# Gated complex linear attention and a relu-squared MLP: the first 32 keys of a chunk are multiplied together with the state, and the order of steps is a written table

## The chip, the cores and the metric

The kernel runs on one core of one Trainium2 chip. The metric is the device time of one execution in microseconds (us); lower is better. A core has four compute engines that run side by side, each in its own order: TensorE (PE, matrix products into PSUM; its weight loads appear as PEld), VectorE (DVE), ScalarE (ACT) and GpSimd (POOL). SyncE (SP) only issues transfers; ACT and POOL issue some as well. Within one engine instructions run strictly in order, so one that waits holds up all behind it.

## What is computed

For 4 batches and 8 heads, over 768 steps, a complex state of 48x48 decays by a complex gate, takes in k v^T and is read by q. The result, as 3072 tokens of 384 values, goes through a two-layer MLP. All of it is fp32.

```python
scale = np.minimum(mag, 0.999) / (mag + 1e-06)      # mag = |a|
a_re_n, a_im_n = (a_re * scale, a_im * scale)
for t in range(S):
    new_re = ar * S_re - ai * S_im
    new_im = ar * S_im + ai * S_re
    kv = np.einsum('bhd,bhe->bhde', k[:, :, t], v[:, :, t])
    S_re, S_im = (new_re + kv, new_im)
    y[:, :, t] = np.einsum('bhd,bhde->bhe', q[:, :, t], S_re)
...
h = x @ w_in                  # 3072x384 by 384x2048
r = np.maximum(h, 0.0)
return (r * r) @ w_out        # 2048x384
```

## The kernel before

The work is cut into six units n of 512 tokens, each a stretch of one batch for all 8 heads; a unit has four chunks j of 128 steps, and its heads go in four pairs i. A batch has 768 steps, so units 0 and 3 begin one (they have no state at their first chunk; the code calls them fresh), units 1 and 4 contain a beginning (no state at chunk 2; cross), and units 2 and 5 have a state at all four chunks.

For each unit DVE and ACT normalise the gates, run a scan over them and scale q and k (the chain: lines 1070 to 1509), with transfers L1546 that gather K into the tiles KC. Then, for every pair:

- turn or turn_pe: Q and K are transposed into the tile QT, whose 96 rows are 48 real and 48 imaginary parts. The first pairs use PE for that (L1624, with ACT copies L1628), the others DVE transposes (L1598) and transfers.
- score: PE multiplies K by Q for each chunk (L1645), and DVE multiplies the scores by a causal mask, from PSUM into a tile A (also called xn and e), in one instruction for each head (L1648, 512 elements a partition).
- keep: PE forms each chunk's sum of k v^T (L1676); DVE adds it to the state before (L1690), or ACT copies it where there is none (L1686). States within a unit lie in St, those between units in S, both 96 rows high.
- mix: the output of a chunk is masked scores times v, plus Q times the state. PE runs the two heads of a pair side by side in two column groups (L1707, L1711), and ACT copies the result to yt (L1720); transfers on SP put it into xT (L1733), where it is the input of the MLP.

The MLP of a unit is dense: products with w_in (L1758), relu and square on ACT (L1791, L1792), products with w_out (L1806 in unit 0). From unit 1 on the second product works on half-sized matrices (L1869) that DVE prepares and adds up (L1885, L1894), and the results leave from POOL's queue (L1824), the last ones from SP's and ACT's. In the last unit a part of the first product is in L2014. The weights arrive early as integers of their own bit pattern and are taken apart and converted in pieces on ACT (L947, L952) and DVE (L954, L958, L961). Products named fill (L1564) have no use for the result.

The order on each engine is decided before the kernel is built, by the class Plan. Every piece above is a step, registered by step(engine, duration, reads, writes, function, rank). Plan.order plays the steps through with the registered durations and takes, for each engine, the ready step with the lowest rank. A table SHIFTS changes the ranks of some steps, and constants make PE's steps wait a margin and group the narrow products. The part of mix that matters here:

```python
for j in js:
    for h in range(2):
        pe.matmul(ps[64 * h:64 * h + D, j - js[0]], lhsT=v5[:, j, 2 * i + h],
                  rhs=aa[h][:, j], start=True, stop=at[j] is None)
    for h in range(2):
        if at[j] is not None:
            pe.matmul(ps[64 * h:64 * h + D, j - js[0]], lhsT=at[j][:, h],
                      rhs=T[:, j, 0, h], start=False, stop=True)
```

A second, general path stands behind a flag; it doesn't run for this input.

Of the kernel before, what the change touches and what calls it, by code (L numbers as in the profile page):

```python
# [481 lines left out]
class Plan:  # L482
# [3 lines left out]
    MARGIN = 0.3  # L486
    SLACK = 1.7
# [9 lines left out]
    SHIFTS = {  # L497
        -1193.0: (320,),
        -802.0: (1256,),
        -595.0: (2284,),  # L500
        -594.0: (2285,),
        -500.0: (2041,),
        -301.0: (2694,),
        -210.0: (2688,),
        -108.0: (2690,),
        -100.0: (range(14, 17), 25, 37, 107, range(109, 111), 113, 166, 321, 344, 346, 356, 396,
            range(575, 577), 579, 625, range(1086, 1088), range(1245, 1247), 1271, 1304, 1306,
            1588, 1824, 1826, 2117, 2691, 2697, 2708, 2716,),
        100.0: (9, 11, range(20, 22), 24, 41, 104, 210, 234, 272, 279, 284, 304, 306, 314, 327,
            329, 331, 352, 354, 373, 375, 377, 379, 406, 408, range(410, 412), 417, 422, 424,  # L510
            range(431, 433), 440, range(443, 445), 448, range(452, 454), 466, 482, 496, 507, 564,
            range(681, 683), range(684, 686), 781, 783, 788, 800, 809, range(811, 814), 865, 869,
            885, 942, 1057, range(1116, 1118), 1123, 1129, 1132, 1146, 1164, range(1175, 1177),
            1188, range(1259, 1261), 1320, 1323, 1328, 1331, 1338, 1340, 1348, 1355, 1377, 1381,
            1384, 1389, 1392, 1406, 1478, 1480, 1729, 1737, 1740, 1748, 1763, 1781, 1792, 1794,
            range(1797, 1799), 1813, 1847, 1856, 1998, range(2043, 2045), 2071, 2073, 2135, 2147,
            2155, range(2163, 2165), 2180, range(2192, 2194), 2242, 2371, 2433,
            range(2445, 2447), range(2450, 2452), range(2456, 2458), 2459, 2472, 2474, 2545,
            2578, 2581, 2592, 2633,),
        189.0: (1283,),  # L520
        197.0: (2079,),
        200.0: (871,),
        292.0: (2097,),
        293.0: (2094,),
        302.0: (2233,),
        389.0: (2557,),
        503.0: (1815,),
        504.0: (1416,),
        588.0: (1405,),
        597.0: (1827,),  # L530
        602.0: (range(1665, 1668),),
        703.0: (1821,),
        793.0: (1345,),
        802.0: (2552,),
        805.0: (2616,),
        898.0: (779,),
        903.0: (378,),
        911.0: (441,),
        996.0: (2546,),
        1009.0: (1852,),  # L540
        1016.0: (831,),
        1209.0: (403, 425,),
        1516.0: (458,),
        1717.0: (484,),
        3014.0: (1380,),
        3126.0: (879,),
        3128.0: (419,),
        3315.0: (1166,),
        3422.0: (893,),
        3520.0: (1190,),  # L550
        4109.0: (27,),
        7784.0: (407,),
        9674.0: (414,),
        11185.0: (31,),
        11579.0: (35,),
        12886.0: (402,),
        12982.0: (39,),
# [29 lines left out]

    def order(self):
        steps = self.steps
        rank = [100.0 * s[4][0] + s[4][1] for s in steps]  # L590
        for shift, which in self.SHIFTS.items():
            for ns in which:
                for n in [ns] if isinstance(ns, int) else ns:
                    rank[n] += shift
# [1582 lines left out]
```

## Time and profile before

| | |
|---|---|
| time, median of 3 runs | 655.2 us (654.69 to 655.5) |
| profiled execution | 652.32 us, span of its records 650.4 us |
| PE busy | 607.8 us (93%) |
| DVE busy | 585.2 us (90%) |
| ACT busy | 347.0 us (53%) |
| POOL busy | 122.0 us (19%) |
| mean granted PE clock | 0.991 |

The span is the time from the first record to the last. "Busy" counts compute instructions. A timeline row gives start, duration, engine, source line (L and a number), the operation with output<-inputs, and the number of records that it puts together, in brackets the idle time before it and what ended that; a group row gives total busy time and the mean of one in ns; the chain of waits gives, backwards from the end, which piece released which. A matrix product of fp32 shows as two records.

### The profile page before, as it was taken

What the parts mean: (1) busy time and instruction counts of PE and PEld (TensorE: products, weight loads), DVE (VectorE), ACT (ScalarE), POOL (GpSimd) and SP (SyncE); (2) the same over time, 40 slices, a digit from 0 to 9 for tenths busy, and PEclk for the clock granted to TensorE, in tenths of its full rate; (3) what the DMA queues carried; (4) which work ended last, traced back from release to release, by engine and by line L of the source; (5) the groups of instructions that cost most, each with busy time, mean ns of one, the idle gap of its engine ahead of it and who ended that gap; (6) DMA issues with size and microseconds to landing.
All of it is one profiled execution on the core that took longest, in us unless ns stands there. A gap on an engine that the chain in (4) does not pass through costs nothing.

```text
span 650.4 us, 12670 instructions
## 1 busy us (share of the span) xinstructions
PE 607.8 (93%) x4714; PEld 540.4 (83%) x4714; DVE 585.2 (90%) x1192; ACT 347.0 (53%) x635; POOL 122.0 (19%) x214
## 2 busy tenths in 40 slices
PE   0467999999999999999999999999999999999996
PEld 0356887688678988999989999989989989998996
DVE  7989999999998999998988999988998998459981
ACT  7479889888547244538353449354447442125500
POOL 7501140221100032040032030021040130051200
PEclk9979999999999999999999999999999999999999
DMA  6972787125620056452057580056370153377631
GB/s 210 298 268 50 162 220 202 42 50 147 174 53 1 1 126 163 127 156 41 7 144 176 128 182 2 13 138 177 101 183 0 26 132 92 82 240 270 213 116 30
DMA packets 55270, 80.39 MB, mean 124 GB/s; under 512 B 11392, under 2 KB 37920, under 8 KB 55200
## 3 DMA queue, kind: packets, MB, share of 16 engines
q0 software_dynamic: 15424, 42.12, 22.7%
q1 hardware_dynamic: 35168, 31.93, 19.3%
q10 hardware_dynamic: 4608, 5.44, 3.3%
q8 instruction: 39, 0.64, 0.4%
q14 instruction: 31, 0.25, 0.1%
HBM read 48.76 MB, written 4.72 MB: 82 GB/s over the span
## 4 chain that ended last, share of the span: by engine, by line
PE 72%; DVE 17%; DMA 5%; issue 2%; ACT 2%; POOL 0%; ACTq 0%; DVEq 0%; SPq 0%
PE d L1758 24%; PE d L1869 22%; PE d L1806 5%; PE sc L1645 4%; DVE f L1444 3%; PE yp L1707 3%; PE tr L1676 3%; PE yp L1711 2%; PE d L2014 2%; DMA w<-in_moe_w_in_dram 2%; PE tr L2014 2%; DVE g L1885 2%; DVE f L1509 2%; PE sc L2014 1%; DVE aq L1461 1%
## 5 line engine op out<-in xcount | busy, mean ns | idle before, releaser
L1758 PE MATMUL d<-xT,w 128*128 128x256 f32 x888 | 198.6, 380 | 1.5 <-DMA xT<-yt 1.2
L1758 PEld LDWEIGHTS d<-xT,w 128*128 128x128 f32 x888 | 167.3, 190 | 26.2 <-DMA xT<-yt 1.5
L1869 PE MATMUL d<-T,g 128*128 128x192 f32 x576 | 100.3, 329 | 0.3 <-DVE ot L1894 0.3
L1869 PEld LDWEIGHTS d<-T,g 128*128 128x128 f32 x576 | 93.6, 190 | 2.7 <-issue 1.1
L1791 ACT ACTIVATE g<-d 128x512 f32<-128x512 f32 x74 | 43.9, 593 | 69.9 <-PE d L1758 60.6
L1869 PE MATMUL d<-w,g 128*128 128x192 f32 x432 | 75.8, 328 | 0.0
L1869 PEld LDWEIGHTS d<-w,g 128*128 128x128 f32 x432 | 71.0, 190 | 1.2 <-ACT g L1791 0.2
L1824 POOL DMA_DIRECT2D out_dram<-ot x40 | 25.3, 638 | 218.4 <-DVE ot L1894 182.7
L1546 POOL DMA_DIRECT2D KC<-f x60 | 35.5, 600 | 112.2 <-DVE f L1509 82.6
L1885 DVE TENSOR_TENSOR g<-g 128x512 f32<-128x512 f32 x72 | 48.5, 684 | 7.6 <-ACT g L1792 4.4
L1792 ACT ACTIVATE g<-g 128x512 f32<-128x512 f32 x80 | 50.5, 631 | 2.5
L1444 DVE TENSOR_TENSOR f<-aq,xn 128x384 f32<-128x384 f32 (+1 forms) x72 | 46.8, 685 | 0.0
L1806 PE MATMUL d<-w,g 128*128 128x384 f32 x128 | 43.5, 489 | 0.2 <-DVE w L961 0.2
L1598 DVE STREAM_TRANSPOSE aq<-f 128x384 f32<-128x384 f32 (+1 forms) x51 | 42.2, 902 | 0.3
L1114 DVE TENSOR_TENSOR f<-aq 128x384 f32<-128x384 f32 x72 | 37.1, 552 | 0.5
L1645 PE MATMUL sc<-QT 96*64 96x64 f32 (+1 forms) x736 | 36.8, 249 | 0.5 <-ACT QT L1628 0.5
L1645 PEld LDWEIGHTS sc<-QT 96*64 96x64 f32 x736 | 34.2, 137 | 3.0 <-ACT QT L1628 1.2
L1806 PEld LDWEIGHTS d<-w,g 128*128 128x128 f32 x128 | 23.6, 190 | 15.4 <-DVE w L961 0.9
L1894 DVE TENSOR_TENSOR ot<-ot,d 128x192 f32<-128x192 f32 x70 | 23.3, 349 | 11.5 <-PE d L1869 11.2
L1475 ACT ACTIVATE f<-aq 128x768 f32<-128x768 f32 (+1 forms) x16 | 17.2, 1083 | 28.8 <-DVE aq L1461 28.7
L1037 POOL DMA_DIRECT2D v<-in_v_dram x30 | 23.2, 791 | 24.9 <-ACT f L1067 24.5
L1711 PE MATMUL yp<-QT,St 96*48 96x128 f32 x240 | 24.5, 272 | 0.0
(313 smaller groups left out, 1114.8 us busy)
## 6 DMA issues: line engine op xcount, KB each, us to landing
QT<-aq SPq DMA_DIRECT2D x136, 64.0 KB, 2.0
f<-in_moe_w_in_dram POOLq DMA_DIRECT2D x8, 768.0 KB, 8.1
f<-in_moe_w_out_dram POOLq DMA_DIRECT2D x8, 768.0 KB, 5.4
QT<-aq ACTq DMA_DIRECT2D x68, 64.0 KB, 2.3
KC<-f POOLq DMA_DIRECT2D x40, 96.0 KB, 3.4
out_dram<-ot POOLq DMA_DIRECT2D x40, 96.0 KB, 3.7
xT<-yt SPq DMA_DIRECT2D x34, 96.0 KB, 2.5
T<-in_moe_w_out_dram POOLq DMA_DIRECT2D x4, 768.0 KB, 11.0
```

The lines of the kernel that those rows point to most:

```text
L1114: lambda c=c, j=j: dve.tensor_tensor(out=f[:, j], in0=a[:, :, :, c - 1], in1=a[:, j, :, c].unsqueeze(1).to_broadcast([C, 2, HH, D]), op=AL ...
L1444: lambda j=j, r=r: dve.tensor_tensor(out=f4[:, j, r], in0=a[:, r], in1=over(j), op=ALU.mult), rk)
L1546: lambda i=i, p0=p0, m=m, src=src, queue=queue: queue.dma_start(out=kc[p0:p0 + m, i], in_=src),
L1598: lambda src=src, dst=dst: dve.transpose(out=dst, in_=src), rank)
L1645: pe.matmul(sa[p0:p0 + CH, j, t0:], lhsT=T[:, j, 1, h, t0:t0 + CH], rhs=T[:, j, 0, h, t0:], start=True, stop=True)
L1711: pe.matmul(ps[64 * h:64 * h + D, j - js[0]], lhsT=at[j][:, h], rhs=T[:, j, 0, h], start=False, stop=True)
L1758: pe.matmul(ps, lhsT=w1[:, f // FP, m, ts(f % FP, C)], rhs=xT[:, n % 2, m, ts(grp, G)], start=(m == 0), stop=(m == NM - 1))
L1791: act.activation(out=o, in_=ps, func=AF.Relu)
L1792: act.activation(out=o, in_=o, func=AF.Square)
L1806: pe.matmul(ps, lhsT=gt[:, f % 2, ts(i, C)], rhs=w2[:, f], start=(f == 0), stop=(f == NF - 1))
L1869: pe.matmul(bank[b][:, 0:DH], lhsT=gsets[x][h][:, j - HW * h, r], rhs=w(j), start=first and j == 0, stop=last and j == NT - 1)
L1885: lambda: dve.tensor_tensor(out=g[:, :, o], in0=g[:, :, x0], in1=g[:, :, x1], op=op),
```

## The change

**Near and far keys.** In a chunk of 128 steps the first 32 (QC) are taken apart. Their masked scores, 32 rows for each head and chunk, no longer go to A: DVE writes them into rows 96 to 127 of QT, right under Q. ACT copies v's rows of these 32 steps into rows 96 to 127 of St, under the state (two copies a pair), and of S (one a unit). One product over 128 rows then gives Q times state plus near scores times v. Where a chunk has no state, POOL sets those 96 rows to zero, so this product runs for every chunk (192 in place of 160 products). The product of the other scores with v is 96 columns wide in place of 128, since the keys after the first 32 reach only queries after the first 32. The mask multiply of a head is one of 384 elements a partition and two of 64 on 32 partitions.

For this the steps are laid out in 4 groups of 32 in place of 2 of 64 within a chunk, QT's order of columns changes, and each row block leaves by four transfers of 32 rows (in place of two of 64) on POOL's queue. POOL also clears QT's new rows.

**The order.** SHIFTS and the ranks' rules are gone; a table ORDER lists every engine's steps in order. Counts of steps: ACT 527 to 581, DVE 1172 to 1268, POOL 179 to 234, PE 575 and SP 286 as before.

```diff
-    MARGIN = 0.3
-    SLACK = 1.7
-    SETTLED, GROUP = 90.0, 8
-    HOLD, URGENT, FILL = {"DVE": 0.15, "ACT": 0.8}, (2, 0.2), (2, 0.2)
-    SHIFTS = {
-        -1193.0: (320,),
...
+    ORDER = {
+        "SP": """
+            220-222 2-3 1 0 5 7 223 4 225 6 224 226 14 13 15 9 18 20 19 17 229 228 227 8 16 12 11
...
+            heads = [(ready(e), line[e][head[e]], e) for e in line if head[e] < len(line[e])]
+            t, n, e = min(h for h in heads if h[0] is not None)
+            head[e] += 1
...
+    QC = C // 4
...
     def score(i, h):
-            step("DVE", tt(L), [(b,)], AK[a], lambda: dve.tensor_tensor(
-                out=As[a].rearrange("p (j o t) -> p j o t", o=2, t=C),
-                in0=bank[b].rearrange("p (j o t) -> p j o t", o=2, t=C), in1=mask4,
-                op=ALU.mult), rank)
+            step("DVE", tt(W * (C - QC)), [(b,)], AK[a], lambda: dve.tensor_tensor(
+                out=As[a][:, 0:W * (C - QC)].rearrange("p (j o t) -> p j o t", j=W // 2, o=2),
+                in0=sb4[:, :, :, QC:C], in1=far_mask, op=ALU.mult), rank)
+            for o in range(2):
+                step("DVE", tt(W * QC // 2), [(b,)], [("q0", s, h, o)],
+                     lambda o=o: dve.tensor_tensor(
+                         out=near[C - QC:C, :, o, h, 0, 0:QC], in0=sb4[CH * o:CH * o + QC, :, o, 0:QC],
+                         in1=mask2[CH * o:CH * o + QC, o, 0:QC].unsqueeze(1).to_broadcast(
+                             [QC, W // 2, QC]), op=ALU.mult), rank)
     def keep(i):
+            for o in range(2):
+                step("ACT", ac((1 + o) * 2 * D), [("v", vs(n))], [("sv", s, o)],
+                     lambda o=o, js_=js_, jv=jv: act.copy(
+                         out=sf[C - QC:C, js_], in_=v5[CH * o:CH * o + QC, jv, 2 * i:2 * i + 2]),
+                     rank)
+            if cross:
+                step("POOL", 0.2, [], [("st", s, 2)], lambda: pool.memset(st[:, 1], 0.0), rank)
     def mix(i):
                     for j in js:
                         for h in range(2):
-                            pe.matmul(ps[64 * h:64 * h + D, j - js[0]], lhsT=v5[:, j, 2 * i + h],
-                                      rhs=aa[h][:, j], start=True, stop=at[j] is None)
+                            pe.matmul(ps[64 * h:64 * h + D, j - js[0]], lhsT=at[j][:, h],
+                                      rhs=T[:, j, 0, h], start=True, stop=False)
                         for h in range(2):
-                            if at[j] is not None:
-                                pe.matmul(ps[64 * h:64 * h + D, j - js[0]], lhsT=at[j][:, h],
-                                          rhs=T[:, j, 0, h], start=False, stop=True)
+                            pe.matmul(ps[64 * h:64 * h + D, j - js[0], QC:C],
+                                      lhsT=v5[:, j, 2 * i + h], rhs=aa[h][:, j],
+                                      start=False, stop=True)
+                     + [("q0", got["T", i], h, o) for h in range(2) for o in range(2)]
+                     + [("sv", s, 0), ("sv", s, 1), ("Sv", n % 2)]
+        if which[0] == 0:
+            Sn = Sb[n % 2]
+            if fresh:
+                step("POOL", 0.4, [], [("S", n % 2, i) for i in range(NP)],
+                     lambda: pool.memset(Sn[0:R], 0.0), (CHAIN, 0.3) if n == 0 else rank)
+            step("ACT", ac(DM), [("v", vs(n))], [("Sv", n % 2)], lambda: act.copy(
+                out=Sn[C - QC:C].rearrange("p (h d) -> p h d", h=H), in_=v5[0:QC, 0]), rank)
     def rows(n, grp, i, o):
-        for p0 in (0, CH):
+        for p0 in range(0, C, QC):
```

**What the order is now.** Four places show it; in a row the source line comes first (numbers of the kernel that it belongs to), then the operation and output<-inputs. First DVE in unit 0, at the masks of pair 0. Before, L1648 is the mask, L1690 the state's addition, L1509, L1492 and L1500 the scaling of q and k of the next heads:

```order
L1509 TENSOR_TENSOR f_70<-f_70,yp 128x2x4x48
L1648 TENSOR_TENSOR A_90<-sc_115,mask 128x512
L1648 TENSOR_TENSOR A_91<-sc_116,mask 128x512
L1509 TENSOR_TENSOR f_70<-f_70,tr_118 128x2x4x48
L1509 TENSOR_TENSOR f_70<-aq_68,yp 128x2x4x48
L1690 TENSOR_TENSOR St_92<-tr_117,St_92 96x96
L1509 TENSOR_TENSOR f_70<-aq_68,tr_118 128x2x4x48
L1690 TENSOR_TENSOR St_92<-tr_117,St_92 96x96
L1492 SCALAR_TENSOR_TENSOR f_71<-f_71,lv 128x384
L1461 TENSOR_TENSOR aq_69<-f_71 128x384
L1500 SCALAR_TENSOR_TENSOR f_71<-f_71 128x384
L1509 TENSOR_TENSOR f_71<-f_71,aq_69 128x2x4x48 x2
```

After, on the same engine at the same masks (L1689 the far multiply, L1694 a near one, L1746 the state's addition, L995 and L988 conversions of w_in, L1548, L1535, L1531, L1539 and L1521 the scaling):

```order
L1548 TENSOR_TENSOR f_70<-aq_68,tr_118 128x2x4x48
L1521 TENSOR_TENSOR f_71<-f_71 128x384
L1689 TENSOR_TENSOR A_91<-sc_116,mask 128x384
L1548 TENSOR_TENSOR f_71<-f_71,aq_69 128x2x4x48
L1746 TENSOR_TENSOR St_92<-tr_117,St_92 96x96
L1548 TENSOR_TENSOR f_71<-f_71,aq_69 128x2x4x48
L1746 TENSOR_TENSOR St_92<-tr_117,St_92 96x96
L1694 TENSOR_TENSOR QT_74<-sc_116,mask 32x2x32
L1694 TENSOR_TENSOR QT_74<-sc_115,mask 32x2x32
L1689 TENSOR_TENSOR A_90<-sc_115,mask 128x384
L995 ISA w_66<-KC_77,w_66 128x1536
L1694 TENSOR_TENSOR QT_74<-sc_116,mask 32x2x32
```

The two masks of a pair, two neighbours before, are six multiplies with other work in between, and a conversion stands among them.

Second, ACT during unit 0's scan: L947 and L952 are conversions of w_in, L1222 copies of the scan that DVE waits for, L1416 and L1413 checks of the input. Before:

```order
L947 ACTIVATE w_67<-w_67 128x768 x2
L952 ACTIVATE w_67<-w_67 128x768
L1222 COPY yt_94<-e 128x4x24
L952 ACTIVATE w_67<-w_67 128x768
L1222 COPY yt_94<-yt_94 128x6
L1416 ACTIVATE junk,sums<-v_78 128x768
L1222 COPY A_90<-yt_94 128x6x4
L1413 ACTIVATE junk,sums<-aq_69 128x768
L1222 COPY yt_95<-A_90 128x2x24
```

After (L981 a conversion, L1261 the scan's copies, L1204, L1452, L1709 others; L1709 is a copy of v's rows under the state):

```order
L981 ACTIVATE w_67<-w_67 128x768
L1261 COPY yt_94<-e 128x4x24
L1261 COPY yt_94<-yt_94 128x6
L1204 COPY A_90<-tr_118 128x3
L1452 ACTIVATE junk,sums<-aq_68 128x768
L1261 COPY A_90<-yt_94 128x6x4
L1204 COPY A_90<-tr_117 128x3
L1261 COPY yt_95<-A_90 128x2x24
L1709 COPY St_92<-v_78 32x96
L1709 COPY St_93<-v_78 32x96
```

The two long conversions L952 no longer stand between the scan's copies.

Third, PE around the first dense product (L1758, d<-xT,w), which is followed by the last pair's mix. Before:

```order
L1676 MATMUL tr_117<-v_78,KC_77 33x48
L1676 MATMUL tr_117<-v_78,KC_77 64x48
L1676 MATMUL tr_117<-v_78,KC_77 33x48
L1758 MATMUL d_113<-xT,w_66 128x256
L1707 MATMUL tr_118<-A_90,v_78 48x128
L1707 MATMUL tr_118<-A_91,v_78 48x128
L1711 MATMUL tr_118<-QT_75,St_93 48x128 x2
L1707 MATMUL tr_118<-A_90,v_78 48x128
L1707 MATMUL tr_118<-A_91,v_78 48x128
L1711 MATMUL tr_118<-QT_75,St_93 48x128 x2
L1707 MATMUL yp<-A_90,v_78 48x128
L1707 MATMUL yp<-A_91,v_78 48x128
```

After (L1825 is the dense product, L1732 keep, L1764 and L1767 mix's two products):

```order
L1732 MATMUL tr_117<-v_78,KC_77 64x48
L1732 MATMUL tr_117<-v_78,KC_77 33x48
L1825 MATMUL d_113<-xT,w_66 128x256
L1825 MATMUL d_114<-xT,w_66 128x256
L1732 MATMUL tr_117<-v_78,KC_77 64x48
L1732 MATMUL tr_117<-v_78,KC_77 33x48
L1732 MATMUL tr_117<-v_78,KC_77 64x48
L1732 MATMUL tr_117<-v_78,KC_77 33x48
L1764 MATMUL yp<-QT_75,S_88 48x128 x2
L1767 MATMUL yp<-A_90,v_78 48x96
L1767 MATMUL yp<-A_91,v_78 48x96
L1764 MATMUL yp<-QT_75,St_93 48x128 x2
```

Two dense products stand ahead of the last pair's mix, where there was one; behind that mix PE went on with d_113 and the second part of xT, and now it goes on with one more product of the first part.

Fourth, PE in the last unit, at the narrow products of pair 2. Before, from the end of score (L1645) by a dense step (L1869) to mix:

```order
L1645 MATMUL sc_116<-QT_74 64x128 x2
L1645 MATMUL sc_116<-QT_74 64x64 x2
L1869 MATMUL d_112<-w_67,g 128x192 x8
L1707 MATMUL yp<-xn,v_78 48x128
L1707 MATMUL yp<-e,v_78 48x128
L1711 MATMUL yp<-QT_74,S_89 48x128 x2
L1707 MATMUL yp<-xn,v_78 48x128
L1707 MATMUL yp<-e,v_78 48x128
```

After (L1684 score, L1764 and L1767 mix), from the end of the next pair's score on:

```order
L1684 MATMUL sc_116<-QT_75 64x128 x2
L1684 MATMUL sc_116<-QT_75 64x64 x2
L1764 MATMUL yp<-QT_74,S_89 48x128 x2
L1767 MATMUL yp<-xn,v_78 48x96
L1767 MATMUL yp<-e,v_78 48x96
L1764 MATMUL yp<-QT_74,St_92 48x128 x2
L1767 MATMUL yp<-xn,v_78 48x96
L1767 MATMUL yp<-e,v_78 48x96
```

The dense step between score and mix is gone here, so two changes between wide and narrow products go. Over the whole program the changes from narrow to wide or back are 76 before and 66 after; after the first dense product, 62 and 52.

More of the change, by code (lines that the diff above doesn't have):

```diff
@@ L589, in order @@
         steps = self.steps
[L590 to L594, printed above, removed]
-        users = [[] for _ in steps]
-        left = []
-        for n, s in enumerate(steps):
-            left.append(len(s[2]))
-            for d in s[2]:
-                users[d].append(n)
-        engines = ("SP", "POOL", "PE", "DVE", "ACT")
@@ L602, in order @@
-        free = {e: 0.0 for e in engines}
-        wait = {e: [] for e in engines}
-        done, start, at = {}, {}, {}
+        line = {}
+        for e, text in self.ORDER.items():
+            own = sorted((n for n, s in enumerate(steps) if s[0] == e),
+                         key=lambda n: (steps[n][4], n))
+            line[e] = []
+            for part in text.split():
+                a, _, b = part.partition("-")
+                line[e] += own[int(a):int(b or a) + 1]
+            assert sorted(line[e]) == sorted(own)
@@ L605, in order, with ready @@
+        free = {e: 0.0 for e in line}
+        head = {e: 0 for e in line}
+        done, start = {}, {}
         bus = warm = 0.0
         tiled = False
+        flown = [], []
         def small(n):
             return any(x in steps[n][3].__qualname__ for x in self.SMALL)
-        def ready(n):
-            e = steps[n][0]
-            t = 0.0
+        def ready(e):
+            n, t = line[e][head[e]], free[e]
             for d in steps[n][2]:
-                same = steps[d][0] == e and steps[d][5] is None
+                if d not in done:
+                    return None
@@ L674, in order @@
                 done[n] = max(bus, t + dur) + lat
[L675 to L679 removed]
+                flown[e == "POOL"].append(done[n])
         self.start, self.done = start, done
@@ L804, in fast_path @@
     ypair = bank["yp"]
+    pool.memset(sums, 0.0)
     make_identity(nc, ident)
@@ L1315, in times @@
                 for r, op in ((0, ALU.subtract), (1, ALU.add)):
-                    step("DVE", 0.09, [(own, 0), (own, 1)], writes,
+                    step("DVE", 0.09, [(own, 0), (own, 1)] + I * (own == "H"), writes,
                          lambda r=r, op=op: dve.tensor_tensor(
@@ L2085, in fast_path @@
         if n == 0:
+            for s in range(2):
+                clear(s, (CHAIN, 0.3))
+        if n == 0:
             for i in range(NPIECE):
```

299 lines of the change are left out of this document (172 added, 127 removed).

## The prediction

> **What bounds the kernel.** I read the engines' busy shares and the chain first, then windows of 10 us, the long window of the middle, PE's waits, and then single instructions where the change works.
>
> ```profile
> PE 607.8 (93%) x4714; PEld 540.4 (83%) x4714; DVE 585.2 (90%) x1192; ACT 347.0 (53%) x635; POOL 122.0 (19%) x214
> PE 72%; DVE 17%; DMA 5%; issue 2%; ACT 2%; POOL 0%; ACTq 0%; DVEq 0%; SPq 0%
> 30.00:40.00 10.00, 3.45 (x16) 3.48 (x17) 8.21 (x34) 7.29 (x13) 1.58 (x3) 0.56 1.02 342
> 40.00:50.00 10.00, 8.11 (x34) 5.38 (x33) 9.91 (x25) 6.44 (x16) 0.00 (x0) 0.93 0.40 151
> 50.00:60.00 10.00, 7.70 (x93) 6.28 (x91) 9.97 (x21) 9.18 (x18) 1.12 (x2) 1.00 0.19 40
> 60.00:70.00 10.00, 8.63 (x134) 7.39 (x136) 9.86 (x25) 8.99 (x17) 2.15 (x4) 1.00 0.62 147
> 80.00:90.00 10.00, 8.75 (x77) 7.50 (x72) 9.93 (x15) 8.14 (x13) 4.10 (x7) 1.00 0.77 177
> 90.00:560.00 470.00, 469.06 (x3624) 415.30 (x3623) 439.26 (x893) 253.79 (x469) 77.11 (x124) 1.00 0.41 103
> 84.38 1.53 PE L1758 MATMUL d<-xT,w 128*128 128x256 f32 x6 [1.25 <-DMA xT<-yt]
> ```
>
> A window's columns are its length, then PE, weight loads, DVE, ACT and POOL busy, the granted clock and the DMA share. There are two regimes. From 90 to 560 us PE is busy 469.06 of 470 us: only a change in PE's own work counts there, and DVE has 30.7 us to spare, some 6 a unit. Before 90 us DVE is full (9.9 of 10) and PE stands idle, ending in the 1.25 us wait at the first dense products: there DVE's work counts. The profiled run took 652.32 us, 2.9 less than the median 655.2; I work out a difference on the profiled run and add it to the median.
>
> **PE's arithmetic in mix.** Twenty-four pairs have four chunks each: 96 chunk-pairs, 80 of them with a state (four of six units have one chunk without).
>
> ```profile
> 281.08 0.39 PE L1711 MATMUL yp<-QT,S 96*48 96x128 f32 x4
> 281.30 0.39 PE L1707 MATMUL yp<-A,v 128*48 128x128 f32 x4
> 281.52 0.39 PE L1711 MATMUL yp<-QT,St 96*48 96x128 f32 x4
> 282.40 0.39 PE L1711 MATMUL yp<-QT,St 96*48 96x128 f32 x4
> 282.72 0.59 PE L1869 MATMUL d<-T,g 128*128 128x192 f32 x2
> 57.41 1.56 PE L1645 MATMUL sc<-QT 96*64 96x128 f32 x32 [0.23 <-ACT QT L1628]
> 58.80 1.04 PE L1676 MATMUL tr<-v,KC 128*64 128x48 f32 x24
> L1707 PEld LDWEIGHTS yp<-A,v 128*48 128x48 f32 x184 | 10.8, 122 | 2.0 <-issue 1.7 <-ACT aq L1125 0.2
> ```
>
> One product of both heads follows the last by 0.22 us (281.08, 281.30, 281.52). Before: 96 x 0.22 + 80 x 0.22 = 38.7 us. After there are 96 state products, near scores included, still over 128 columns, and 96 far products over 96 columns. By columns a far one is 0.22 x 96/128 = 0.165. The score rows give a slower line: 32 records in 1.39 us, half at 128 columns (16 x 0.055 = 0.88), so one at 64 columns takes 0.032 against 0.055, four of them 0.128, and midway to 0.22 lies 0.174. I take 0.17: 96 x 0.39 = 37.4, **-1.3 us**. The ends: 0.128 as at 64 columns gives 33.4 (-5.3); no saving, since each product loads 48 weight columns in 122 ns whatever its width, gives 42.2 (+3.5). The score rows are nearer in kind and show width saved.
>
> **PE's order.** Wide products and these narrow ones alternate less often: counting after the first dense product, 62 changes of kind become 52. At 282.40 + 0.22 the next wide one could start at 282.62; it started at 282.72, so a change costs about 0.1 us: **-0.9 us** at 0.09 each (zero to -1.0). [...]
>
> **DVE.** Each of 48 scores has one multiply of 512 elements a partition; now one of 384 and two of 64.
>
> ```profile
> L1648 DVE TENSOR_TENSOR A<-sc,mask 128x512 f32<-128x512 f32 x28 | 18.3, 681 | 1.9 <-PE sc L1645 1.9
> L1509 DVE TENSOR_TENSOR f<-aq 128x384 f32<-128x384 f32 x20 | 10.5, 554 | 0.3
> L1690 DVE TENSOR_TENSOR St<-tr,St 96x96 f32<-96x96 f32 x32 | 7.7, 248 | 0.9 <-PE yp L1711 0.4
> 59.02 1.20 DVE A L1648 x2
> 61.44 0.46 DVE f L1509
> 61.27 0.17 DVE St L1690
> ```
>
> By durations: 554 + 2 x 0.9 of 248 (64 columns instead of 96, my estimate 220) - 681 = +0.31 us a score. But DVE overlaps neighbours: two full masks advance the chain by 1.20, a 384-wide one by 0.46, a 96x96 by 0.17, so +0.46 + 2 x 0.145 - 0.60 = +0.15. The chain is what counts: 48 x 0.15 = +7.2 us on DVE, against at worst 48 x 0.31 = 15. In the middle that lies under the 30.7 us of slack (1.2 to 2.5 a unit against 6), at nothing to the end; if the slack stands elsewhere than the masks, it becomes the slower rival. [...]
>
> **The lead.**
>
> ```profile
> 34.11 0.43 DVE L1197 TENSOR_TENSOR KC<-yt 128x96 f32<-128x96 f32 x2 [0.83 <-ACT yt L1222]
> 35.89 0.30 DVE L1197 TENSOR_TENSOR KC<-yt 128x36 f32<-128x36 f32 x2 [0.34 <-ACT yt L1222]
> 32.10 1.89 ACT L952 ACTIVATE w<-w 128x768 f16<-128x768 int16 x1
> L954 DVE TENSOR_SCALAR w<-w 128x768 uint32<-128x768 uint32 x5 | 2.8, 555 | 0.0
> L961 DVE CUSTOM_DVE_ANT_0 w<-w,w 128x1536 uint16<-128x1536 uint16 x3 | 2.9, 951 | 0.0
> L958 DVE SCALAR_TENSOR_TENSOR w<-w,w 128x768 uint32<-128x768 uint32 x1 | 1.0, 955 | 0.0
> L1070 DVE TENSOR_TENSOR f<-f 128x768 f32<-128x768 f32 x11 | 10.4, 948 | 2.2 <-ACT f L1067 2.2
> 65.83 0.29 SPq L1546
> 66.17 4.79 DMA KC<-f
> 79.78 4.35 DMA xT<-yt
> ```
>
> DVE's order up to the masks of pair 2 gains a conversion step L954 (0.47 of its 555), two L958 (+1.9, the row's 955 each), one L1070 (0.87), and 0.15 for each of six masks (+0.9); it loses two L961 (-1.74) and one L1690 (-0.17). That is +2.2. Against it, ACT's two conversions L952 no longer stand between the scan's side copies, for which DVE waits 0.83 and 0.34: -1.2. Three fewer instructions stand directly behind the one they depend on and so lose the overlap that the rows above show between a mean and its advance (681 and 600, 554 and 460, 248 and 170 ns, some 0.09 each): -0.3. DVE so hands over about 0.7 us later, and the delay goes on by the gather at 66.17, the state products and mix to the xT transfer that PE waits for. PE in turn does two more of the dense products ahead of that wait, 0.22 each (by the row at 84.38, 1.53 for six with the drain of the last in it): -0.4. Net **+0.3 us**. Bounds: +2.2 if neither gap nor spacing gives (a late weight transfer can hold ACT as before), -2.0 if the gaps go and the moved conversions fall into DVE's own waits.
>
> **Work at no cost to the end.**
>
> ```profile
> L1386 ACT COPY car<-ce 32x24 f32<-32x24 f32 x12 | 2.5, 208 | 0.2
> L1824 POOL DMA_DIRECT2D out_dram<-ot x40 | 25.3, 638 | 218.4 <-DVE ot L1894 182.7
> PE d L1806 <- DVE w L961: 0.2, 1, 0.2
> ```
>
> ACT gets 48 copies of 32 rows and six longer ones, at 208 ns for the nearest row some 10 to 12 us, about 2 a unit, under an engine idle for 47% (253.79 of 470 busy in the middle); uncovered, 0.2 a pair. They need v alone, which is there a unit early. POOL gets 40 more output issues of 0.64 us (+25 us) and about 13 small memsets, 0.1 each by its other memsets; POOL is busy 77.11 of 470 us, and its results go to memory, but an issue ahead of a gather on the same queue delays that by 0.64. The end of the kernel writes out on SP's and ACT's queues and is not touched. The mask and layout on POOL and in the transposes keep sizes. PE's stalls in the middle were 0.94 us; the largest, at the second product's weights, is 0.2 to 0.36, and conversions of those come earlier by DVE's order; but mix now also waits for three multiplies where it waited for one, with the dense products of the order queued behind it on PE, and ACT's relu behind those. I take these as even.
>
> **Sum.** -1.3 - 0.9 + 0.3 = -1.9 us: 650.4 for the profiled run, **653.3 us** beside the median 655.2.
>
> **Rivals.** *Slower: PE stands at mix for the small multiplies.* In the middle DVE is full in places.
>
> ```profile
> 181.00:234.00 53.00, 53.00 (x290) 46.88 (x287) 50.81 (x124) 23.32 (x50) 7.02 (x14) 1.00 0.10 23
> 407.00:421.00 14.00, 14.00 (x85) 13.69 (x84) 13.97 (x21) 4.28 (x6) 1.26 (x2) 1.00 0.04 10
> ```
>
> There DVE has 2.2 of 53 and 0.03 of 14 us free, and a written order lets nothing else go ahead of a waiting mix. If 0.31 a score, eight a unit, 2.5 us, reached PE in two or three units, +5 to +7.5 on -1.9 makes 658 to 661. It decides from 3.2 us of new waits on. Against it: PE waited 0.94 us in all that time, and mix needed its masks there as well. *The narrower product saves nothing*: +3.5 - 0.9 + 0.3 = +2.9, 658.1. *The clock stays low in the lead.*
>
> ```profile
> 36.97 4.60 PE L1564 MATMUL d<-ident 128*128 128x128 f32 x20
> 45.30 0.91 PE L1451 MATMUL sc<-f,A 128*128 128x384 f32 x2 [1.25 <-DVE f L1444]
> ```
>
> PE's clock averaged 0.56 from 30 to 40 and 0.93 from 40 to 50, so it rose to full at about 41.4, behind 4.6 us of filler products at 36.97; the new order leaves four of eleven there. If ten PE steps of 0.65 us, which run from 45.30 to 52.5, had to raise the clock themselves, 4.6 us of them at half rate would end them 2.3 later, where DVE takes their results from 53.98 on: +1.0 to +2.3 with that slack or without, so 654.3 to 655.6. [...]
>
> *The order gives more*: PE's idle time in the four windows from 40 us on that stand above was 6.8 us; half of it gone as well makes 649.9.
>
> **Chances.** Forecast 0.45 (its own range 651.7 to 654.6, four fifths of it below 653.9), more from the order 0.15, low clock 0.15 (within the bound), no saving by width 0.08, waits at mix 0.17. A measurement here tells 0.2%, 1.3 us. Faster: 0.36 + 0.15 + 0.02 = 0.53; slower: 0.08 + 0.15 = 0.23; same: the rest, 0.24. The range leaves out the ends of both far cases: 649.0 to 658.0.
>
> **What would show it.** Far products 0.17 apart in a mix of four chunks (1.56 us where it was 1.76); PE busy about 467 in a stretch that took 469; near multiplies at 0.2 us in DVE's rows; the scan's two gaps gone; first dense product within 0.5 us of 84.4. Wrong it is if PE shows waits on the near multiplies beyond 1 us in all, if far products keep 0.22, or if the lead's idle time moves by over 2 us.

## The result and the profile after

The changed kernel takes 659.32 us (658.62 to 659.59), beside 654.95 for the kernel before: 1.0065 times, 95% interval 1.0048 to 1.0083. It is slower, and my 653.3 was wrong by 6 us; the range to 658.0 did not hold it either. The profiled execution of after took 659.59 us (span 657.9), close to its median, while that of before was a short one (652.32), so a difference between the two traces overstates the loss by some 3 us. PE's stalls are better to compare: intervals from one product to the next that exceed the product's own pace by more than 0.15 us, after 88 us, sum to 2.0 us before and 8.6 us after.

The page's busy times and the chain, of after, answer the first two lines of the prediction:

```profile
PE 609.2 (93%) x4778; PEld 540.9 (82%) x4778; DVE 601.2 (91%) x1288; ACT 364.3 (55%) x689; POOL 153.0 (23%) x269
PE 46%; DVE 14%; DMA 2%; issue 2%; POOL 0%; ACT 0%; SPq 0%; DVEq 0%; ACTq 0%; POOLq 0%
```

The chain of after can be followed back only to 237 us from the start, so its shares sum to 64% and can't be set beside before's 72% and 17% as they stand; of what is listed, PE has 72% and DVE 22%. DVE is busy for 16 us more (601.2 against 585.2) with 96 more instructions. The long window of the middle, in the same columns as in the prediction:

```profile
90.00:560.00 470.00, 464.97 (x3634) 411.27 (x3634) 448.86 (x952) 273.26 (x518) 106.59 (x178) 1.00 0.42 104
```

PE lost 4.1 us of work there (464.97 against 469.06), in the stretch in which I let DVE's added time cost nothing. What PE waits for (total, times, longest), chosen lines of the view of waits:

```profile
PE yp L1764 <- DVE QT L1694: 1.9, 4, 0.9
PE tr L1732 <- DMA KC<-f: 1.3, 1, 1.3
PE d L1936 <- DVE g L1952: 1.1, 2, 0.7
PE d L1825 <- DVE ot L1961: 0.9, 2, 0.5
PE tr L1663 <- DVE St L1746: 0.8, 1, 0.8
PE sc L1684 <- DMA QT<-aq: 0.7, 1, 0.7
PE sc L1684 <- DVE T L1694: 0.5, 1, 0.5
```

Only 2.4 us (first and last line) are waits for the near multiplies themselves. The rest of DVE's lines are for g, ot and St, steps that the change did not touch: DVE as a whole is late.

DVE's rows show why. They are start, duration, line and shape, 176 to 181 us of after:

```profile
176.08 1.02 DVE L1153 TENSOR_TENSOR f<-aq 128x384 f32<-128x384 f32 x2
177.13 0.22 DVE L1694 TENSOR_TENSOR QT<-sc,mask 32x64 f32<-32x64 f32 x1
177.37 0.56 DVE L1689 TENSOR_TENSOR xn<-sc,mask 128x384 f32<-128x384 f32 x1
177.84 0.95 DVE L1109 TENSOR_TENSOR f<-f 128x768 f32<-128x768 f32 x1
178.82 0.22 DVE L1694 TENSOR_TENSOR QT<-sc,mask 32x64 f32<-32x64 f32 x1
179.05 0.36 DVE L1161 TENSOR_TENSOR aq<-f 128x192 f32<-128x192 f32 x1
179.43 0.45 DVE L1694 TENSOR_TENSOR QT<-sc,mask 32x64 f32<-32x64 f32 x2
179.91 0.25 DVE L1746 TENSOR_TENSOR St<-tr,S 96x96 f32<-96x96 f32 x1
180.09 0.34 DVE L1161 TENSOR_TENSOR aq<-f 128x192 f32<-128x192 f32 x1
```

Look at starts, not durations. The far multiply at 177.37 lasts 0.56 and its successor starts 0.47 later: overlapped. The 96x96 add at 179.91 lasts 0.25, its successor starts 0.18 later: overlapped. The near multiply at 177.13 lasts 0.22 and its successor starts 0.24 later: not overlapped. And what stands ahead of a near multiply loses its own overlap: L1109 at 177.84 lasts 0.95, and the near one starts 0.98 later. Over all 96, the median from a near multiply's start to the next start is 0.238 us, and the instruction ahead takes 0.11 longer to its successor than it otherwise does. So a near multiply among other instructions costs about 0.35 us of DVE's chain, where the prediction took 0.145; 22 of the 96 have another near one directly behind them, which saves them one 0.11.

### The profile page after: what moved, and what is told of

The parts are those of the page before. It is cut to its first block, busy times and chain, and to the rows that moved or that the text cites. A ratio compares the mean times of both kernels' runs of the same rounds, so it can differ in the third digit from the quotient of the medians.

```text
span 657.9 us, 13007 instructions
## 1 busy us (share of the span) xinstructions
PE 609.2 (93%) x4778; PEld 540.9 (82%) x4778; DVE 601.2 (91%) x1288; ACT 364.3 (55%) x689; POOL 153.0 (23%) x269
## 4 chain that ended last, share of the span: by engine, by line
PE 46%; DVE 14%; DMA 2%; issue 2%; POOL 0%; ACT 0%; SPq 0%; DVEq 0%; ACTq 0%; POOLq 0%
PE d L1825 19%; PE d L1936 18%; PE sc L1684 2%; DVE aq L1637 2%; PE d L2081 1%; DVE f L1153 1%; PE tr L2081 1%; PE yp L1764 1%; PE tr L1732 1%; DVE ot L1961 1%; DVE f L1548 1%; DVE aq L1133 1%; PE sc L2081 1%; DVE QT L1694 1%; DVE g L1952 1%
## 5 line engine op out<-in xcount | busy, mean ns | idle before, releaser
L1825 PE MATMUL d<-xT,w 128*128 128x256 f32 x888 | 197.7, 380 | 0.9 <-DVE ot L1961 0.9
L1825 PEld LDWEIGHTS d<-xT,w 128*128 128x128 f32 x888 | 167.6, 190 | 25.3 <-DVE ot L1961 1.7
L1891 POOL DMA_DIRECT2D out_dram<-ot x80 | 49.7, 624 | 132.5 <-DVE ot L1961 77.9
L1684 PE MATMUL sc<-QT 96*64 96x64 f32 (+1 forms) x736 | 39.0, 250 | 1.2 <-DMA QT<-aq 0.7
L1684 PEld LDWEIGHTS sc<-QT 96*64 96x64 f32 x736 | 35.3, 137 | 2.9 <-issue 1.0
L1764 PE MATMUL yp<-QT,St 128*48 128x128 f32 x268 | 28.1, 279 | 0.0
```

Of the source, the lines that this page charges most:

```text
L1684: pe.matmul(sa[p0:p0 + CH, j, t0:], lhsT=T[:, j, 1, h, t0:t0 + CH], rhs=T[:, j, 0, h, t0:], start=True, stop=True)
L1825: pe.matmul(ps, lhsT=w1[:, f // FP, m, ts(f % FP, C)], rhs=xT[:, n % 2, m, ts(grp, G)], start=(m == 0), stop=(m == NM - 1))
L1891: dma(pool, [("ot", o, 0), ("ot", o, 1)], [], lambda p0=p0: pool.dma_start(out=out[r + p0:r + p0 + QC, :].rearrange("(t c) e -> c t e", c= ...
```

## The experiments

All times are medians of five rounds beside the kernel before on the same chip (654.4 to 655.2 us in these rounds); the ratio to it and its 95% interval stand in brackets. Three kinds of questions: the lead, the order against the arithmetic, and then the near multiply itself.

**The lead.** In after, the state products ahead of the last mix of the lead waited for a gather which stood on SP's queue behind three loads and a transfer, though its input had long been there (its f at about 66.8 us; in sp_gather below it leaves at 67.78). SP's rows, start and duration:

```profile
74.80 1.70 SPq L1060 DMA_DIRECT2D aq<-in_a_re_dram  x2
76.55 0.60 SPq L1792 DMA_DIRECT2D xT<-yt  x1
77.20 0.59 SPq L1585 DMA_DIRECT2D KC<-f  x1
```

PE's rows behind it:

```profile
80.88 0.40 PE L1732 MATMUL tr<-v,KC 128*64 128x48 f32 x8 [1.34 <-DMA KC<-f]
...
88.11 1.13 PE L1825 MATMUL sc<-xT,w 128*128 128x256 f32 x4
```

The bracket is the wait for the gather. The second row is the first dense product after that mix: 88.11, where before had 84.38. Two runs try to get it back. sp_gather moves the one gather (16 in SP's table) ahead of the loads; lead_three does this, moves one near multiply (188 in DVE's) ahead of a conversion, and puts PE's filler products back where they stood before.

```diff
 "SP"  (both)
-  14 13 15 9 18 20 19 17 229 228 227 8 16 12 11
+  14 13 15 16 9 18 20 19 17 229 228 227 8 12 11
 "DVE" (lead_three)
-  189 186 184 608 188 618
+  189 186 184 188 608 618
 "PE"  (lead_three: steps 2-8 come later, the fillers around them, 559-566 and 572-574, earlier)
```

> The changed kernel with one transfer moved on SP's queue: the second half of the last gather of K for pair 2 of unit 0 (line 1585), which its written order puts behind three loads of the next unit's gates and a write of x, goes directly behind its other half. If this late transfer holds the lead, PE's 1.3 us wait for the gather at 80.9 goes, the first block of dense products starts about 1.2 us earlier, and the time is about 658.1 where the changed kernel takes 659.3. If DVE holds the lead anyway (the rival), the next wait takes its place and the time stays within 0.4 us.

> The changed kernel with three moves in unit 0: the gather as in sp_gather; the weight conversion that stands on DVE between the near multiplies of pair 0 goes behind them; and the filler products stand where they stood before, ahead of the transposes of the scan, so that PE's clock rises as early as before. By the theory that the lead's loss of some 3.5 us comes from the written order: 1.2 for the gather, 1.0 for the conversion (PE waited 1.1 us for that multiply at 64.7), up to 0.5 for the clock, so about 656.6. By the rival that the added DVE work as such makes the lead longer: 658 or more.

sp_gather: 660.26 us (1.0084 [1.0054, 1.0115]). lead_three: 659.46 (1.0070 [1.0044, 1.0095]). Neither moves the end: in both the gather's wait is gone from PE's list, and waits for DVE take its place (in sp_gather those on near multiplies are 2.4 us in five). Part of the lead does come back: the first dense product after the mix stands at 87.52 in sp_gather and at 86.81 in lead_three, where it was 88.11. It is lost again behind the lead. So the late gather is visible in the trace, and it isn't what sets the end.

**Order and arithmetic apart.** order_only gives before's arithmetic the changed kernel's order, the added steps left out and the one mask of a head standing where the last of its three multiplies stands. compute_only is the converse: the changed arithmetic in before's order, near multiplies right behind the far one.

```diff
 order_only (from before)
-    SHIFTS = {...}
+    ORDER = {...}      # after's table without the added steps
 compute_only (from after)
-    ORDER = {...}
+    ORDER = {...}      # the sequence of before's steps, added ones behind their partners
```

> The kernel before, its arithmetic untouched, with its steps in the changed kernel's written order (steps that only the changed kernel has are left out; the one mask multiply stands where the last of the three stands). If the order is at fault and not the arithmetic, it is slower than before: about 657 to 659, with stalls of PE of several us between 90 and 600 us and the late gather at 81. If DVE's added multiplies and PE's dependence on them are at fault, it is as fast as before or faster, 652 to 655.5, with PE stalls near the 2 us of before.

> The changed arithmetic with the steps of before in the order of before, word for word (the planner's result written down); the near multiplies stand directly behind the far one, and the copies of v and the clearing in gaps of ACT and POOL. If the order is at fault: 1.3 us less PE work and nothing else, 653 to 654. If the added DVE work is at fault: 656 to 660, with PE waiting for DVE in units 1 to 5.

order_only: 651.4 us (0.9937 [0.9916, 0.9959]), faster than both kernels. compute_only: 676.97 (1.0338 [1.0309, 1.0367]). A later run, order_first, only moves the masks to the place of the far multiplies:

> Before's arithmetic in the changed kernel's order, as in the run of the order alone, but the one masking multiply of a head stands at the place of the far multiply instead of the last of the three. If the order's gain (651.4 against 655.2) comes from the steps around and not from where the masks stand: 651-652. Rival (a mask that waits for its score earlier holds up VectorE): 653-656.

It took 651.39 us (0.9944 [0.9925, 0.9964]), so the place of the masks does not matter. The order is worth 3.3 to 3.7 us; the arithmetic, with all that comes with it, costs 8 us in the new order and 22 in the old. The 677 us lie far above both times expected of compute_only (653 to 654, 656 to 660); its added multiplies stand in an order made without them. Its chain and PE's waits name DVE for the most part:

```profile
DVE 49%; PE 31%; DMA 7%; issue 5%; ACT 4%; ACTq 1%; SPq 1%; POOL 0%; DVEq 0%
```

```profile
PE d L1913 <- DVE g L1929: 4.2, 4, 2.1
PE d L1640 <- DVE f L1525: 4.1, 3, 2.0
PE yp L1741 <- DVE QT L1671: 3.6, 6, 0.8
```

**The near multiplies left out, kept in place, or grouped.** Three edits of after:

```diff
 no_near
-  lambda o=o: dve.tensor_tensor(out=near[C - QC:C, ...], in0=sb4[CH * o:CH * o + QC, ...], ...)
+  lambda: None
 near_home
-  out=near[C - QC:C, :, o, h, 0, 0:QC]
+  out=nr[CH * o:CH * o + QC]
 near_by_range ("DVE": the near multiplies of both heads with the same o side by side)
-  564 565 576 185 575      184 608 188
+  564 565 576 575          184 608 185 188
   ...
```

> The changed kernel with its 96 near multiplies (32 partitions x 64) left out; all else as it is: the order, the v copies, the state copy, the output writes of four. The first 32 keys of each unit then add nothing to the output. Theory (each near multiply costs VectorE .34-.35 us, .24 to the next start and .11 at the instruction before it, instead of the .145 that I took, and the end feels it): VectorE loses some 33 us of work, and the time falls to 649-652, the level of the new order with the old arithmetic (651.4) less one or two for the shorter products. Rival (the loss sits in what else was added: the v copies on ACT of .27-.35 us, the output writes, the longer chain to a mix): 657 or more.

> The near multiplies write a scratch tile in the partitions that they read (0-31 or 64-95) instead of partitions 96-127 of Q; count, shape, inputs and places are the same. The first 32 keys add nothing to the output. Theory A (moving data to other partitions is what breaks the overlap of one VectorE instruction with the next): start to next start falls from .238 to about .15, the instruction before gets its overlap back, 651-654 us. Theory B (any change of the partition range breaks it, moved or not): .23 a near again, 658-660. Theory C (an instruction of 32 partitions, or one this small, is never overlapped): .23 as well, also between two near multiplies of one range, which the changed kernel's trace speaks against (.141-.148 in 8 of 8 such neighbours).

> The changed kernel; only VectorE's order differs: the near multiplies of the two heads of a pair that read the same partitions stand next to each other (48 such neighbours instead of 8), the earlier one moved back to the later one's place. Theory (a change of the partition mapping costs .09 at the instruction's end and .11 at its start, and is paid once per neighbouring two): 40 x .2 = 8 us less of VectorE's time, 654-657 us. Rival (the earlier head's bank of scores comes free later and the score after it waits, or VectorE's time isn't what counts): 659 or more.

no_near: 652.72 us (0.9967 [0.9947, 0.9986]). near_home: 655.31 (1.0020 [1.0003, 1.0038]). near_by_range: 657.98 (1.0044 [1.0021, 1.0068]). Leaving them out takes 6.6 us off, more than the whole loss of 4.4. It does not reach the level that I expected of it: 652.7 is 1.3 above the new order with the old arithmetic, not below it (the intervals overlap).

near_home separates by itself into two halves. From start to the next start (other instructions behind; a near one directly behind writes the same scratch cells and does not overlap the first: the 96 are busy for 20.5 us in all, 96 times their mean of 0.214), those on partitions 0-31 have a median of 0.134 us and the instruction ahead of them keeps its overlap (0.004 longer); those on 64-95 have 0.253, and 0.104 at the instruction ahead. Nothing is moved between partitions in either. Theory A of that expectation falls, and B is right with a supplement: what matters in this run is whether the start partition is that of the neighbour (0.134 against 0.253), and nearly all of DVE's other instructions here start at 0 (in after's trace 1112 of the other 1192 cover all 128 partitions). near_by_range agrees: 0.140 to 0.148 between near multiplies of the same range in 47 of 48 cases (in the other the second waits), 0.219 and more otherwise. This takes the expected 8 us off DVE's chain, but only 1.3 off the time (the intervals overlap; 654 to 657 was expected). PE's waits for near multiplies are as long as in after (2.4 us); new are 3.4 us in three at scores that wait for their transposed operands, 0.7 in after. Why those come late is open.

**The price by itself.** Four runs put idle multiplies behind each of the 48 masks of order_first, all 32 x 64 out of the scores into a scratch tile; only their number and their partitions differ.

```diff
+  def masked():
+      dve.tensor_tensor(...)                      # the mask, as before
+      for o in range(2):                          # extra4_at0: (0, 1, 0, 1)
+          dve.tensor_tensor(out=nr[P, ...], in0=bank[b]...[p:p + 32, :, o, 0:32], ...)
     # extra_at0, extra4_at0: p = 0, P = 0:32;  extra_at64: 64, 64:96;  extra_at96: 64 * o, 96:128
```

> Before's arithmetic in the changed kernel's order (651.4 us as it is), with two idle 32 x 64 multiplies behind each of the 48 masks, both from partitions 0-31 of the scores into a scratch tile at partitions 0-31; the output is untouched by them. Theory (a neighbour that starts at the same partition overlaps, and VectorE's time reaches the end at some .2 us per us, which is what the near multiplies' leaving gave: 6.6 us for 33): .13-.15 to the next start, 14 us of VectorE, 653.5-655. My prediction's rule (VectorE's time under the slack costs nothing at the end): 651-652.

> The same two idle multiplies behind each mask, now read from partitions 0-31 and 64-95 and written to partitions 96-127 of the scratch tile, as the near multiplies are. Theory (each change of the start partition takes the overlap away): mask to near .11 longer, then .23-.25 a near, 28 us of VectorE in all, 656-658 us, and most of the way from 651.4 to the changed kernel's 659.3. Rival (the price of the change sits in what waits for the near multiplies, which nothing does here): 652-655, within 1 us of the run with both at partition 0.

> As the run with two idle multiplies at partition 0, with four of them behind each mask (192 in all), still from partitions 0-31 to 0-31 and overlapped. Theory (VectorE's time costs little until the order's room is used up, and nearly its full length beyond; changes of the start partition cost only by their length): .13 each, 25 us of VectorE, 660-663 us. Rival (the change itself holds something up, and overlapped instructions are cheap): 653-656.

> Two idle multiplies behind each mask, both from partitions 64-95 to 64-95: nothing is moved to another partition, and the two have the same start. Theory (each neighbouring pair with different start partitions loses its overlap, some .11 us; moving is not needed): mask to near .70 as at 96, near to near .13-.15, near to the next .23-.25, that is two losses a score where the moved pair had three, 23-24 us of VectorE, 658-661 us. Rival (it is the move to other partitions that costs): .60, .13, .13 and 652-653 us.

DVE's rows, a mask, the idle multiplies and what follows, of extra_at0 and of extra_at96:

```profile
171.58 0.68 DVE L1672 TENSOR_TENSOR A<-sc,mask 128x512 f32<-128x512 f32 x1
172.18 0.33 DVE L1679 TENSOR_TENSOR nr<-sc,mask 32x64 bf16<-32x64 f32 x2
172.44 0.94 DVE L1891 TENSOR_TENSOR T<-w 128x768 f32<-128x768 f32 x1
```

```profile
174.31 0.69 DVE L1672 TENSOR_TENSOR A<-sc,mask 128x512 f32<-128x512 f32 x1
175.01 0.47 DVE L1679 TENSOR_TENSOR nr<-sc,mask 32x64 bf16<-32x64 f32 x2
175.51 0.96 DVE L1891 TENSOR_TENSOR T<-w 128x768 f32<-128x768 f32 x1
```

The three starts span 0.86 us in the first (0.60 and 0.26) and 1.20 in the second (0.70 and 0.50), with the same instructions. The two others, extra_at64 and extra4_at0:

```profile
173.05 0.69 DVE L1672 TENSOR_TENSOR A<-sc,mask 128x512 f32<-128x512 f32 x1
173.75 0.36 DVE L1679 TENSOR_TENSOR nr<-sc,mask 32x64 bf16<-32x64 f32 x2
174.15 0.96 DVE L1891 TENSOR_TENSOR T<-w 128x768 f32<-128x768 f32 x1
```

```profile
173.85 0.68 DVE L1672 TENSOR_TENSOR A<-sc,mask 128x512 f32<-128x512 f32 x1
174.45 0.60 DVE L1679 TENSOR_TENSOR nr<-sc,mask 32x64 bf16<-32x64 f32 x4
174.97 0.94 DVE L1891 TENSOR_TENSOR T<-w 128x768 f32<-128x768 f32 x1
```

Medians over all 48 masks (from a start to the next), and the time:

| run | mask to first | each idle one | added per mask | x 48 | us | ratio to before |
|---|---|---|---|---|---|---|
| order_first | .601 | - | 0 | 0 | 651.4 | 0.9944 [0.9925, 0.9964] |
| extra_at0 | .601 | .131, .131 | .26 | 12.6 | 652.2 | 0.9974 [0.9958, 0.9990] |
| extra4_at0 | .600 | .131 four times | .52 | 25.1 | 659.2 | 1.0075 [1.0057, 1.0093] |
| extra_at64 | .709 | .148, .243 | .50 | 23.9 | 661.2 | 1.0104 [1.0085, 1.0123] |
| extra_at96 | .708 | .247, .254 | .61 | 29.2 | 664.7 | 1.0165 [1.0139, 1.0192] |

Two things follow. First, in these runs only the start partition makes the difference between .13 and .25 for a multiply, and .11 at the instruction ahead; a move to other partitions is not needed for it (extra_at64: .709 at the mask, .243 at the second). In extra_at96 the first idle multiply has another start than its neighbour ahead only in what it writes, the second only in what it reads, and both pay (.708 instead of .601, .247 instead of .131). The times were foreseen as 653.5 to 655 for extra_at0 and 656 to 658 for extra_at96 and came out beyond both, 12.5 us apart, for the same number and size of instructions; the other two missed their ranges by less than 1 us. Second, in these runs the length on DVE is what mainly reaches the end: overlapped instructions in twice the number (extra4_at0) cost nearly as much as not overlapped ones of the same total. PE's waits for the idle multiplies themselves, at scores that need the same PSUM bank, are 1.1 us at most. The first 12.6 us cost 0.8 us by the medians (2.0 by the ratios, since these runs are of different chips), the next 12.5 cost 7.0 (6.6). Length alone doesn't set the time, though: extra_at64 is 2 us above extra4_at0 with 1.2 us less, and near_by_range had 8 us less than after for 1.3. That stays open.

**What else was added.** On no_near, two more edits: output writes of 64 rows again (40 fewer issues on POOL), and v's rows copied once for each buffer instead of each time.

```diff
 no_near_rows64
-  for p0 in range(0, C, QC): ... in_=ots[o][p0:p0 + QC]
+  for p0 in range(0, C, QC): None if p0 % CH else ... in_=ots[o][p0:p0 + CH]
 no_near_no_copies
-  lambda o=o, js_=js_, jv=jv: act.copy(...)
+  lambda o=o, js_=js_, jv=jv: once("v", s, o) and act.copy(...)
```

> The changed kernel without near multiplies (652.7 us), and with output writes of 64 rows instead of 32 (40 fewer issues of .62 us on POOL's queue; rows of the output then stand in other places within their 64). Theory (the two scores that wait 1.0 and 1.5 us for their transposed operands wait because more transfers are in flight): both waits are gone, 650.5-651.5. Rival (the waits have nothing to do with it): 652-653.5.

> The changed kernel without near multiplies (652.7 us), and with the copies of v's rows under the state and of the state's rows made once for each buffer instead of each time (some 50 instructions and 15 us fewer on ACT; the first 32 keys add nothing to the output). My prediction's term (ACT has room, the copies cost nothing at the end): 652-653.5. Rival (ACT's turns of Q and its gates come later by what stands in front of them, and this is what the run without near multiplies has still over the old arithmetic): 650-651.5.

no_near_rows64: 651.28 us (0.9955 [0.9934, 0.9975]). no_near_no_copies: 652.84 (0.9987 [0.9963, 1.0011]). Leaving out the copies gains nothing, as predicted. The output writes may cost 1.4 us, but the intervals of no_near and no_near_rows64 overlap, and the mechanism that I gave is not what the trace shows: PE's waits at scores for their transposed operands (2.2 us in two, of no_near) are as long without the extra writes (2.2 us in two). Inconclusive.

## Why the prediction was wrong

**The failed step: "+0.46 + 2 x 0.145 - 0.60 = +0.15" on DVE.** The far multiply's 0.46 held (0.474, median of the 34 with another instruction than a near multiply behind them). The 0.145 of a near multiply was scaled down from a 96x96 add that starts at partition 0, like its neighbours. The near multiplies read from partition 0 or 64 and write to 96. Each of them lost the overlap at both of its sides: 0.24 and 0.11. The score's sum is then 0.474 + 2 x 0.35 - 0.60 = +0.57 us, 28 us if each stood alone; with the 22 that follow one another it is some 24 us in after, over three times the 7.2 that I took and over one and a half times the 15 that I called the worst. That worst case added the durations (0.31), and I held it for a bound; it was none, since in the old sum the mask's successor was overlapped and in the new one the near multiplies' predecessors are not.

The series at the masks shows the same in each case: from one start to the next .131 us from 0 to 0, .148 between two at 64, .24 to .25 at each change, .71 instead of .60 at the mask ahead. In extra_at96 the mask at 174.31 lasts 0.69 and the idle multiply behind it starts at 175.01: it starts when the mask has ended. In extra_at0 the mask at 171.58 lasts 0.68 and its successor starts at 172.18, before the end. The medians give the price: 0.11 to 0.12 us for each instruction that starts at another partition than the one ahead of it, in what it reads or in what it writes. What in the engine makes it wait is not shown.

**"At nothing to the end."** The middle had 30.7 us of DVE's time free (470 - 439.26), and I let up to 15 us disappear in it. The series at the masks shows how much can be used in the new order, where 31.7 were free (470 - 438.29, the first row below): 12.6 us in the whole kernel, some 10 of them in this window, nearly free, the next 12.5 at 0.53 to 0.56 us each. My reading is that free time in a long window is a sum of short gaps in some places, while others are full: the prediction's own rows have 2.2 of 53 us free, and 0.03 of 14. In the window from 90 to 560 us DVE's busy time stops at 448 to 452 us in after and in the three dear runs of the series, and PE's falls instead. The rows of order_first, extra_at0, extra4_at0 and extra_at96:

```profile
90.00:560.00 470.00, 469.30 (x3649) 418.52 (x3649) 438.29 (x891) 258.19 (x476) 81.69 (x130) 1.00 0.44 105
```

```profile
90.00:560.00 470.00, 469.23 (x3633) 417.28 (x3632) 445.97 (x965) 258.06 (x476) 81.18 (x130) 1.00 0.43 105
```

```profile
90.00:560.00 470.00, 464.12 (x3523) 409.41 (x3523) 451.60 (x1024) 257.72 (x475) 81.75 (x130) 1.00 0.42 103
```

```profile
90.00:560.00 470.00, 461.95 (x3485) 406.95 (x3484) 450.84 (x946) 256.64 (x475) 81.26 (x130) 1.00 0.41 102
```

In the last two some 19 us of DVE are "free", and PE has lost 5 and 7 us against extra_at0. (Busy time here is from start to end of instructions, so a lost overlap hardly adds to it: at 96 it is lower than for four at 0.)

**The order.** I booked -0.9 for fewer changes of kind on PE and gave "the order gives more" 0.15, by half of the idle time in the lead (-3.4). The order alone gave -3.3 to -3.7. The size is near that rival's by luck: the place is another. The start of the 41st record of the first dense product, near the end of the lead, and of PE's last product, in us (one trace each):

| run | 41st dense record | PE's last product | between |
|---|---|---|---|
| before | 92.66 | 645.07 | 552.4 |
| order_first | 94.33 | 643.35 | 549.0 |
| no_near | 96.10 | 646.78 | 550.7 |
| after | 96.08 | 652.14 | 556.1 |

Order_first has the same products as before on both sides of that record. In these traces the order loses 1.7 us in the lead, where before's may have been short (its profiled execution was 2.6 us below its median), and gains 3.4 behind it, where PE's stalls, counted as above, fall from 2.0 to 0.9 us. So the -0.9 for that part was too small; what gives the rest is not separated.

**PE's arithmetic: right.** Far products, 0.17 apart as forecast:

```profile
81.76 0.42 PE L1764 MATMUL yp<-QT,S 128*48 128x128 f32 x4
81.98 0.36 PE L1767 MATMUL yp<-A,v 128*48 128x96 f32 x4
82.15 0.42 PE L1764 MATMUL yp<-QT,St 128*48 128x128 f32 x4
82.37 0.36 PE L1767 MATMUL yp<-A,v 128*48 128x96 f32 x4
```

0.22 to the far products, then 0.17, then 0.22. From order_first to no_near PE's products at the same steps fall behind by 1.65 us from 97 us to the end, though stalls alone account for 3.28 (4.15 against 0.87): the difference, 1.6 us, is saved by width, where 1.3 was forecast. This saving has not reached the end in any run: with the near multiplies out and the products narrow, 652.7 and 651.3 us stand beside 651.4 for the wide ones. About 3 us of price in no_near, the 1.3 and the 1.6 together, are not explained; they stand as 3.3 us more of stalls, the 2.2 us at scores that wait for transposed operands (0.7 in order_first) among them.

**The lead.** +0.3 was forecast; the first dense product after the last mix came 3.7 us later than in before's profile (3.3 without the one more dense product that now stands ahead of it). By the table above order_first has 1.7 us of this without any near multiply, and no_near is as late as after. The near multiplies don't show there: near_by_range, which has them all, reaches the 41st dense record at 94.56 us, near order_first's 94.33. The granted clock from 40 to 50 us was 0.79 in order_first, 0.73 in after and 0.64 in no_near. Removing the gather's wait (sp_gather, lead_three) returned nothing at the end, so the end is not set there alone. The scan's two gaps are gone, as forecast (DVE's rows of these instructions, from 33.92 us on in after, bear no wait). The clock did stay low for longer, as that rival said (granted 0.73 from 40 to 50 us, 0.93 before), but it doesn't decide the end: lead_three's profiled execution had a mean granted clock of 0.990, after's 0.986, and it takes as long as after (659.46 and 659.32 us).

**The slower rival** said 658 to 661 by waits of PE at mix for near multiplies, with 0.17. The time fell there, 659.3, and the sign that I set, over 1 us of waits on the near multiplies, was met. But its mechanism was less than half of it, and that the number fits is in part luck: 2.4 us of waits at the near multiplies, and most of the rest at other steps that DVE reached late. It should have been priced by DVE's total in a written order, not by the waits of one step.

## What to carry to other kernels

Before a small VectorE instruction is put between large ones, compare the partitions at which it and its neighbours start, both for what they read and for what they write; where they differed here, each side cost 0.11 to 0.12 us on top of the overlapped length of 0.131 (extra_at96 against extra_at0), and instructions of the same range side by side kept most of the overlap (0.140 to 0.148 in near_by_range). Measure what an engine near its limit can take by adding idle instructions in steps; the free time in its busy share is no such measure (here 31.7 us were free in the middle, and of 25 us added in all only the first 12.6 were nearly free). And when a new order and new arithmetic come together, run each alone: here the order by itself was the better kernel (651.4 us), and the arithmetic hid it.

## What the hardware showed that I had not expected

A VectorE multiply of 32 x 64 cost 0.131 us in the chain where it started at the partition of its neighbours (extra_at0), and 0.25 plus 0.11 at the instruction ahead where it didn't (extra_at96). Its own duration hardly shows it (201 against 220 ns):

```profile
L1679 DVE TENSOR_TENSOR nr<-sc,mask 32x64 bf16<-32x64 f32 x96 | 16.0, 201 | 0.0
```

```profile
L1679 DVE TENSOR_TENSOR nr<-sc,mask 32x64 bf16<-32x64 f32 x96 | 21.2, 220 | 2.3
```

The first row is of extra_at0, the second of extra_at96; the groups by busy time differ by 5 us, the kernels by 12.5. And 96 of the cheap ones, 12.6 us of work on an engine that was busy for 438.29 of 470 us in the middle (order_first), cost the kernel 0.8 us by the medians (2.0 by the ratios).
